# Moving a weight conversion ahead of the silu's low part on VectorE, and the second head's operand casts two steps later

## The chip, the cores and the metric

The kernel runs as one program on one core of one Trainium2 chip. The metric is device time in microseconds (us), the median of three runs. Inside the core five engines work side by side, each through its own instructions in order: TensorE (PE in the profile, with its weight loads as PEld), VectorE (DVE), ScalarE (ACT), GpSimd (POOL) and SyncE (SP). SyncE computes nothing; its line is the queue from which nearly all DMA transfers are issued. One engine waits for another through semaphores.

## The reference

Three parts in a chain, all in 32-bit floats (shapes: batch 2, 8 heads, 768 positions, head size 64; 1536 tokens of width 512):

```
q_bits = (q @ proj > 0);  k_bits = (k @ proj > 0)          # 6 bits each
mask   = bucket(q_bits) == bucket(k_bits)
attn   = softmax(where(mask, q @ k.T / 8, -1e9));  x = attn @ v
h = x @ w_in;  x = (h * sigmoid(h)) @ w_out                # 512 -> 2048 -> 512
tokens with x @ w_skip > 0 go to the best of 8 experts:
    x += gate * (relu(x @ w1[e]) @ w2[e])                   # 512 -> 1024 -> 512
```

## The kernel before, in words

**Split operands.** TensorE multiplies in a rounded 32-bit format. To keep precision a matrix is written as a high part (the rounded value) and a low part (what the rounding lost), and a product is taken as high x high + low x high + high x low. In the MLP a weight piece `wraw` of 128x1024 becomes `whi` (a cast on ScalarE, line 249) and `wlo` (a subtraction on VectorE, line 252).

**Attention.** Heads are worked in eight pairs. A pair has 12 steps, numbered m = 0 to 11 in the code (so the eighth step is m = 7): two halves of the queries ("units"), three blocks of 128 queries in each, two heads for each block, alternating. Step s issues, in order: scores `S` on TensorE (line 391; the operands are K1, K2, Q1, Q2), the first half of the transposes `T` of step s-2 (line 417) with ScalarE's copy `PT` (line 420), the row maximum `mx` and `bs` on VectorE (401, 403), the exponentials `P` on ScalarE (405), the product `pv` with the values (431), and the second half of the transposes with VectorE's copy (422). There are two score buffers, so `S` of step s waits until `P` of step s-2 has read its buffer.

While pair i is worked, the operands of pair i+1 are prepared. Two lists set by hand where: `PRE` (ahead of `P` in the step) and `POST` (at the step's end). For each head (0 or 1) there are six pieces: `kh` and `qa` are casts on ScalarE (lines 317 and 320) that write the high parts; `k2` and `qb` are DMA copies of those parts to the other half of the partitions, issued on SP (lines 312 and 314); `kl` and `ql` are subtractions on GpSimd (325, 330). The first pair has lists of its own (`i == 0`). Pair i+1's step 0 needs head 0, its step 1 needs head 1. SP's queue also carries, in this order: the mask rows (lines 355 and 360), and at each unit's end the round trip of the row sums: `r` written to `r_d` in DRAM (445), read back as `rb` by two broadcasts (448) that wait until that write has landed; then the next values `v` (289) and the raw q and k (283).

`em_r` (line 442) transposes a unit's reciprocal row sums on TensorE as `rT`; it stood at `k == 1`, right behind the second and before the third pair of `pv` products of that unit. For the last unit the VectorE work before it includes the first silu's low part.

**Weights for the MLP.** They arrive as 64-bit numbers and are converted in three steps (`convert`): ScalarE makes `u` (line 214, two pieces), VectorE shifts into `mag` (215, two), and VectorE then does four more passes, two into `mag` (219) and two into `wraw` (223). The first four blocks are converted during attention, in single pieces at steps 4, 9 and 11 of pairs 2 to 5 and in the last steps; blocks 4 to 15 in the MLP's first batch of tokens.

**MLP.** Tokens run in three batches of 512, and each batch over 16 blocks n of the inner width. Block n issues: the split of block n+1 (`whi`, `wlo`) with the start of the conversion of block n+2 (`u`, shift), then `em_h(n)` (12 matmuls into `ph` at line 619, silu `g` and its high part `gh` on ScalarE at 625 and 626, its low part `gl` on VectorE at 627), then the rest of the conversion of block n+2, then `em_out(n-1)` (12 matmuls into `o`, lines 653 and 662). All engines' orders are fixed by the order in which the program writes them; no scheduler moves them.

Of the kernel before, what the change touches and what calls it, by code (L numbers as in the profile page):

```python
# [25 lines left out]
def kernel(  # L26
# [16 lines left out]
    nc = tc.nc  # L43
# [190 lines left out]
    def split(i):  # L234
        assert next(splitting(i), "end") == "end"
# [28 lines left out]
    def attention(hook):  # L264
# [26 lines left out]
        def prep_alloc(i):  # L291
            pl = mainp if i % 2 else evp
            ops[i] = [pl.tile([P, 2, S], F32R, name=n, bufs=1) for n in ("Q1", "K1", "Q2")] + [K2s[i % 2]]
            mks[i] = (topp.tile([P, HQ], F32, name="ma"), topp.tile([P, HQ], F32R, name="mb"))
# [78 lines left out]
        units = [(i, qh) for i in range(B * NP) for qh in range(2)]  # L373
# [6 lines left out]
        def em_S(s, parts=(0, 1)):  # L380
            u, qt, hd = steps[s]
            i, qh = units[u]
            Q1, K1, Q2, K2 = ops[i]
            q0 = qh * HQ + qt * P
            if 0 in parts:
                st_S[s] = psS.tile([P, 2, 512], F32, tag="S", name="S", bufs=2)
            ps = st_S[s]
            for j in parts:
                q_, k_, n, first = ((Q1, K1, P, True), (Q2, K2, NK2, False))[j]
                for c in range(2):  # L390
                    nc.tensor.matmul(ps[:, c, 0:HQ], q_[0:n, hd, q0:q0 + P], k_[0:n, hd, c * HQ:(c + 1) * HQ],  # L391
                                     start=first, stop=not first)
# [33 lines left out]
        def em_PV(u, k):  # L426
            i, qh = units[u]
            if k == 0:
                st_pv[u] = psTV.tile([P, HQ], F32, tag="V", name="pv", bufs=1)
            for hd in range(2):  # L430
                nc.tensor.matmul(st_pv[u][hd * D:(hd + 1) * D], vts[i][:, k, hd], st_PT[u][:, hd, k],  # L431
                                 start=(k == 0), stop=(k == KT - 1))
# [45 lines left out]
        def em_busy(n):  # L478

            for _ in range(n):  # L480
                nc.tensor.matmul(bs, busy[:, 0:P], busy, start=True, stop=True)
# [21 lines left out]
        for j, ps in enumerate(direct):  # L503
# [6 lines left out]
            else:  # L510
# [14 lines left out]
        prep_op(1, 0, "scale", nc.scalar)  # L525
        nc.gpsimd.memset(K2s[1][D:D + 32].bitcast(F32), 0.0)

        PRE = [(1, 0, "kh", nc.scalar), (3, 0, "qa", nc.scalar), (5, 1, "kh", nc.scalar), (7, 1, "qa", nc.scalar)]

        POST = [(1, 0, "k2", None), (2, 0, "kl", nc.gpsimd), (3, 0, "qb", None), (4, 0, "ql", nc.gpsimd),  # L530
                (5, 1, "k2", None), (7, 1, "kl", nc.gpsimd), (7, 1, "qb", None), (9, 1, "ql", nc.gpsimd)]

        PRE, POST = ([ops_, [(x + 2, *op) for x, *op in ops_]] for ops_ in (PRE, POST))
        rbs, xs = {}, {}
        for s in range(NS + PU + 4):
            i, m = divmod(s, 2 * PU)
            nxt = i + 1 < B * NP
            if nxt and m == 0:
                prep_alloc(i + 1)
            if s < NS:  # L540
                em_S(s, (0, 1) if s else (1,))
            if 0 <= s - 2 < NS:
                em_T(s - 2, 0)
            for mm, *op in PRE[i == 0]:
                if nxt and mm == m:
                    prep_op(i + 1, *op)
            w, pm = divmod(s, PU)
            u, k = (w - 1, pm - 2) if pm >= 2 else (w - 2, pm + 4)
            pv = 0 <= u < len(units)

            if pv and k % 2:
                em_PV(u, k - 1)
                em_PV(u, k)
            if s < NS:
                em_soft(s)
            if s == 1:
                prep_op(0, 1, "k2", nc.scalar)
                prep_op(0, 1, "kl", nc.vector)
            if s < 2:
                em_busy(2)  # L560
            if 0 <= s - 2 < NS:
                em_T(s - 2, 1)
            if pv:
                if k == 0:
                    em_rc(u)
                if k == 1:
                    rbs[u] = em_r(u)
                if k == KT - 1:
                    xs[u] = em_out(u)
                if k == 3 and u:  # L570
                    em_x(u - 1, xs.pop(u - 1), rbs.pop(u - 1), nc.gpsimd)
            if nxt:
                if m == (1 if i else 5):
                    prep_proj(i + 1)
                if m == (2 if i else 6):
                    prep_mask(i + 1, nc.gpsimd if i else nc.scalar)
                for mm, *op in POST[i == 0]:
                    if mm == m:
                        prep_op(i + 1, *op)
                if m == (4 if i else 8):  # L580
                    prep_rows(i + 1)
                if m == 0 and i + 2 < B * NP:
                    prep_load(i + 2)
                if m == (9 if i else 11) and i + 2 < B * NP:
                    prep_op(i + 2, 0, "scale", nc.scalar)
                if m == 11 and i + 2 < B * NP:
                    load_v(i + 2)
                if m == 11 and i + 2 == B * NP:
                    top_st.close()
            if s == NS - 2 * PU:  # L590
                ev_st.close()
            hook(s - NS)
            if s == NS - 1:
                psS_st.close()
# [246 lines left out]
    with tc.manual_schedule():  # L841
# [17 lines left out]
        for n in range(N + 1):  # L859
            cv = convert(n + 2) if NEARLY <= n + 2 < NF else iter(())  # L860
            while cnt["spl"] < min(n + (3 if n >= NF else 2), N):

                sp = splitting(cnt["spl"], apart=True)
                next(sp)
                next(cv, None)
                next(sp, None)
            if n >= N - 2:
                while cnt["spl"] < NM + (1 if n == N - 2 else 3) and any(h[1] > 1 for h in homes):
                    split(cnt["spl"])
            if n < N:  # L870
                if n >= len(EARLY_H):
                    em_h(n)
                for _ in cv:
                    pass
            if n == NF - 2:
                pools["stg_st"].close()
                pools["gwb"], gwb_st = opened("gwb", side="right")
                pools["gwb_t"] = pools["gwb"].tile([P, NE + 1, DM], F32, name="gwb")
                nc.sync.dma_start(pools["gwb_t"].rearrange("p c d -> p (c d)"), gr.to_broadcast([P, (NE + 1) * DM]))
            if n == 3:  # L880
                cf = pools["xo"].tile([P, DM], F32, tag="x", name="cf", bufs=6)
                nc.sync.dma_start(cf[:, 0:consts.shape[1] - NC - P], consts[:, NC + P:])
            if n == 6:
                nc.vector.tensor_copy(cb, cf[:, 0:consts.shape[1] - NC - P])
            if n == 1:
                nc.sync.dma_start(tk, tok)
                nc.gpsimd.memset(gwc, 0.0)
                nc.sync.dma_start(gwc[:, :, 0:NE + 1], gw.rearrange("(k p) c -> p k c", p=P))
                z = pools["gwb0"] = sm.tile([P, NE * NTOK // P], F32, name="zid", bufs=1)
                nc.gpsimd.memset(z, float(DUMMY))  # L890
                nc.sync.dma_start(id_d.rearrange("(p r) c -> p (r c)", p=P), z)
                zx = sm.tile([P, DM // P], F32, name="zx", bufs=1)
                nc.gpsimd.memset(zx, 0.0)
                nc.sync.dma_start(x_d[NTOK:NTOK + 1].rearrange("o (p c) -> (o p) c", p=P), zx)
                nc.sync.dma_start(g_d[NTOK:NTOK + 1], zx[0:1, 0:1])
            if n >= 1:
                em_out(n - 1)
                b, f = items[n - 1]
                if f == NF - 1 and b + 1 < len(TILES):
                    todo.extend((t, c) for t in range(*TILES[b]) for c in range(NE + 1))  # L900
            if routing is not None and next(routing, "end") == "end":
                routing = None
            if n % NF:
                for j in range(4):
                    if todo:
                        logit(*todo.pop(0))
                        if not todo:
                            bb = n // NF - 1
                            if idx is None:
                                idx = ps_tile("idx", [P, 3], "O4")  # L910
                            routing = route(*TILES[bb], L[:, TILES[bb][0]:TILES[bb][1]], ps_tile("pr", [P, 512], "X"), idx)
# [49 lines left out]
        for t in range(t1 - t0):  # L961
            x = pools["xo"].tile([P, DM], F32, tag="x", name="x", bufs=6) if t < 2 else ep.tile([P, DM], F32, tag="eo", name="x")
# [280 lines left out]
```

## Time and profile before

| | |
|---|---|
| median of 3 runs | 639.28 us (638.69 to 642.12) |
| the profiled execution's own time | 640.85 us |
| its span, first to last instruction | 639.0 us |
| PE / DVE / ACT / POOL busy | 610.4 / 468.9 / 403.8 / 171.0 us |
| mean granted TensorE clock | 0.997 |

A row of the timeline has the start and the duration in us from the span's start, the engine, the line, the operation, output<-inputs, the count of merged instructions, and in brackets the idle time of the engine before it with what ended it. Matmuls are pipelined, so the next one may start before the modelled end of the last. In such rows the tiles K1 and K2 read `K`, and Q1 and Q2 read `Q`.

### The profile page before, as it was taken

The page shows a single profiled execution, that of the slowest core. Times are in us where ns is not written, and L with a number is a line of the kernel's source. Part 1 is how long each engine was busy: PE and PEld are TensorE (multiplying, and loading weights), DVE is VectorE, ACT ScalarE, POOL GpSimd, SP SyncE. Part 2 cuts the span into 40 slices and gives each one's busy share as a digit, 9 for nine tenths or more (in the row PEclk, how much of TensorE's full clock was granted, in tenths as well). Part 3 has the DMA queues.
Part 4 walks back from the last instruction along what each step waited for, and adds up shares of the span by engine and source line. Part 5 has one row for each costly group of instructions (what it writes and reads, how often), then busy time and mean ns, then how long its engine had stood idle before and what let it go on. Part 6 is the DMA issues. An engine that isn't in the chain of part 4 may idle for free.

```text
span 639.0 us, 9525 instructions
## 1 busy us (share of the span) xinstructions
PE 610.4 (96%) x3239; PEld 461.9 (72%) x3239; DVE 468.9 (73%) x861; ACT 403.8 (63%) x675; POOL 171.0 (27%) x261
## 2 busy tenths in 40 slices
PE   8899999999999999998899999999999988999996
PEld 3667676666767756776678888788887766788885
DVE  6867778788787665778776777447775568899992
ACT  6978788787887984454555333444433456788881
POOL 4437556383744142000000000020000035523201
PEclk9999999999999999999999999999999999999998
DMA  3532542534224124545443000007223258999920
GB/s 109 148 120 64 173 108 82 157 74 129 65 57 105 78 78 114 176 162 168 151 146 148 0 1 2 0 3 197 90 80 128 66 132 224 363 406 406 408 78 27
DMA packets 30978, 83.45 MB, mean 131 GB/s; under 512 B 6032, under 2 KB 9810, under 8 KB 30798
## 3 DMA queue, kind: packets, MB, share of 16 engines
q1 hardware_dynamic: 28834, 79.06, 38.5%
q0 software_dynamic: 1936, 3.65, 1.7%
q8 instruction: 26, 0.43, 0.3%
q14 instruction: 26, 0.21, 0.1%
q10 hardware_dynamic: 156, 0.10, 0.1%
HBM read 67.65 MB, written 8.50 MB: 119 GB/s over the span
## 4 chain that ended last, share of the span: by engine, by line
PE 74%; ACT 9%; DVE 7%; issue 4%; DMA 3%; POOL 1%; SPq 1%; POOLq 0%; DVEq 0%; ACTq 0%
PE ph L619 17%; PE o L662 10%; PE S L391 9%; PE pv L431 9%; PE T L417 8%; PE o L653 7%; PE eh L1059 5%; PE ey L1081 5%; ACT P L405 3%; ACT u L214 2%; DVE mag L219 2%; DVE mx L401 1%; PE tr L1037 1%; DVE wraw L223 1%; ACT K L317 1%
## 5 line engine op out<-in xcount | busy, mean ns | idle before, releaser
L249 ACT CAST whi<-wraw 128x1024 fp32r<-128x1024 f32 x100 | 102.7, 1050 | 45.0 <-DVE wraw L223 38.1
L252 DVE TENSOR_TENSOR wlo<-wraw,whi 128x1024 fp32r<-128x1024 f32 x100 | 119.6, 1222 | 11.5 <-ACT whi L249 10.5
L405 ACT ACTIVATE P<-S,bs 128x768 f32<-128x768 f32 x96 | 95.5, 994 | 26.0 <-DVE bs L403 23.2
L401 DVE TENSOR_REDUCE mx<-S 128x1 f32<-128x768 f32 x96 | 91.1, 949 | 14.2 <-PE S L391 11.8
L391 PE MATMUL S<-K,Q 88*128 88x384 f32 (+1 forms) x384 | 92.5, 362 | 7.8 <-ACT P L405 6.0
L625 ACT ACTIVATE g<-ph 128x512 f32<-128x512 f32 x48 | 28.5, 595 | 107.1 <-PE ph L619 93.7
L417 PEld LDWEIGHTS T<-ident,P 128*128 128x128 f32 x576 | 68.0, 140 | 30.9 <-ACT PT L420 18.6
L627 DVE TENSOR_TENSOR gl<-g,gh 128x512 fp32r<-128x512 f32 x48 | 33.3, 693 | 77.0 <-ACT gh L626 77.0
L417 PE MATMUL T<-ident,P 128*128 128x128 f32 x576 | 88.7, 277 | 0.2 <-ACT PT L420 0.2
L791 POOL DMA_INDIRECT id_d<-tk,slot x12 | 12.1, 1006 | 261.6 <-DVE pre L799 258.5
L391 PEld LDWEIGHTS S<-K,Q 88*128 88x128 f32 (+1 forms) x384 | 63.0, 191 | 16.0 <-ACT P L405 8.8
L431 PE MATMUL pv<-PT,v 128*64 128x384 f32 x384 | 72.5, 499 | 0.0
L422 DVE COPY PT<-T 128x384 f32<-128x384 f32 x85 | 47.0, 553 | 22.0 <-PE T L417 21.3
L619 PE MATMUL ph<-xhi,whi 128*128 128x512 f32 x192 | 54.4, 405 | 6.4 <-ACT whi L249 6.4
L420 ACT COPY PT<-T 128x384 f32<-128x384 f32 x107 | 50.6, 479 | 9.4 <-PE T L417 8.7
L619 PE MATMUL ph<-xlo,whi 128*128 128x512 f32 x192 | 52.3, 394 | 0.0
L619 PE MATMUL ph<-xhi,wlo 128*128 128x512 f32 x192 | 52.1, 393 | 0.0
L619 PEld LDWEIGHTS ph<-xhi,whi 128*128 128x128 f32 x192 | 34.6, 188 | 17.8 <-ACT whi L249 10.6
L675 DVE CUSTOM_DVE_ANT_0 junk<-x,gwb 128x512 bf16<-128x512 f32 x72 | 45.4, 686 | 0.0
L619 PEld LDWEIGHTS ph<-xlo,whi 128*128 128x128 f32 x192 | 36.1, 188 | 8.5
L619 PEld LDWEIGHTS ph<-xhi,wlo 128*128 128x128 f32 x192 | 36.1, 188 | 8.3
L431 PEld LDWEIGHTS pv<-PT,v 128*64 128x64 f32 x384 | 23.3, 136 | 25.5 <-issue 25.2
(177 smaller groups left out, 1049.9 us busy)
## 6 DMA issues: line engine op xcount, KB each, us to landing
wraw<-in_w_dram SPq DMA_DIRECT2D x64, 512.0 KB
w<-in_mw_dram SPq DMA_DIRECT2D x32, 512.0 KB
v<-in_vt_dram SPq DMA_DIRECT2D x8, 384.0 KB
rb<-r_d SPq DMA_DIRECT2D x32, 96.0 KB
out_dram<-x SPq DMA_DIRECT2D x12, 256.0 KB
x_d<-x SPq DMA_DIRECT2D x11, 256.0 KB
raw<-in_kT_dram SPq DMA_DIRECT2D x7, 384.0 KB
raw<-in_qT_dram SPq DMA_DIRECT2D x7, 384.0 KB
```

The lines of the kernel that those rows point to most:

```text
L249: nc.scalar.copy(hi[:, sl], t[:, sl])
L252: eng.tensor_tensor(lo[:, sl], t[:, sl], hi[:, sl].bitcast(F32), op=ALU.subtract)
L391: nc.tensor.matmul(ps[:, c, 0:HQ], q_[0:n, hd, q0:q0 + P], k_[0:n, hd, c * HQ:(c + 1) * HQ], start=first, stop=not first)
L401: nc.vector.tensor_reduce(mx[:, 0:1], ps[:, :, 0:HQ], axis=AX.XY, op=ALU.max, negate=True)
L405: nc.scalar.activation(pt.rearrange("p (a b) -> p a b", a=2), ps[:, :, 0:HQ], AF.Exp, bias=bs_[:, 0:1], scale=bs_[:, 1:2], accum_out=st_su ...
L417: nc.tensor.transpose(ps[:, j], pt[:, k * P:(k + 1) * P], ident)
L420: nc.scalar.copy(dst, ps)
L422: nc.vector.tensor_copy(dst, ps)
L431: nc.tensor.matmul(st_pv[u][hd * D:(hd + 1) * D], vts[i][:, k, hd], st_PT[u][:, hd, k], start=(k == 0), stop=(k == KT - 1))
L619: nc.tensor.matmul(p_[:, 0:c1 - c0], w[:, k * P:(k + 1) * P], x[:, k, t0 * P + c0:t0 * P + c1], start=(q == 0), stop=(q == len(ops3) - 1))
L662: nc.tensor.matmul(acc[t], g[:, (t - t0) * P:(t - t0 + 1) * P], w[:, DM:PIECE], start=(f == 0 and q == 0), stop=(f == NF - 1 and q == 2))
L675: nc.vector.tensor_tensor_reduce(junk, xts[t], pools["gwb_t"][:, c], op0=ALU.mult, op1=ALU.add, scale=1.0, scalar=0.0, accum_out=L[:, t, c ...
```

## The change

```diff
@@ the lists in attention @@
-        PRE = [(1, 0, "kh", nc.scalar), (3, 0, "qa", nc.scalar), (5, 1, "kh", nc.scalar), (7, 1, "qa", nc.scalar)]
+        PRE = [(1, 0, "kh", nc.scalar), (3, 0, "qa", nc.scalar), (7, 1, "kh", nc.scalar), (9, 1, "qa", nc.scalar)]
         POST = [(1, 0, "k2", None), (2, 0, "kl", nc.gpsimd), (3, 0, "qb", None), (4, 0, "ql", nc.gpsimd),
-                (5, 1, "k2", None), (7, 1, "kl", nc.gpsimd), (7, 1, "qb", None), (9, 1, "ql", nc.gpsimd)]
-        PRE, POST = ([ops_, [(x + 2, *op) for x, *op in ops_]] for ops_ in (PRE, POST))
+                (7, 1, "k2", None), (8, 1, "kl", nc.gpsimd), (9, 1, "qb", None), (10, 1, "ql", nc.gpsimd)]
+        PRE, POST = ([ops_, [(x + (1 if x < 5 else -1), *op) for x, *op in ops_]] for ops_ in (PRE, POST))
@@ the step loop @@
-                if k == 1:
+                if k == (1 if u + 1 < len(units) else 3):
                     rbs[u] = em_r(u)
@@ the MLP's loop over blocks @@
             if n < N:
+                for _ in cv:
+                    pass
                 if n >= len(EARLY_H):
                     em_h(n)
-                for _ in cv:
-                    pass
```

From the second pair on, head 1's K cast and copy move from step 5 to step 7 and its Q cast and copy from step 7 to step 9; the GpSimd subtractions move from 7 and 9 to 8 and 10. In the first pair all twelve entries of `PRE` and `POST` move one step earlier, and head 1's `kl` (9 to 7) and `ql` (11 to 9) two. For the last unit `em_r` moves behind the third pair of `pv` products. In the MLP the four remaining conversion passes are written ahead of `em_h`.

VectorE in the MLP's first batch, before: `w_3202` and `w_3252` are the two arrived pieces of one weight block, and the rows run from one block's last conversion passes to the next block's.

```order
L219 SCALAR_TENSOR_TENSOR mag<-u,mag 128x512 x2
L223 SCALAR_TENSOR_TENSOR wraw<-u,mag 128x512 x2
L215 TENSOR_SCALAR mag<-w_3202 128x512
L215 TENSOR_SCALAR mag<-w_3252 128x512
L252 TENSOR_TENSOR wlo<-wraw,whi 128x1024
L627 TENSOR_TENSOR gl<-g,gh 128x512
L219 SCALAR_TENSOR_TENSOR mag<-u,mag 128x512 x2
L223 SCALAR_TENSOR_TENSOR wraw<-u,mag 128x512 x2
```

The same place now; the pieces have other numbers.

```order
L215 TENSOR_SCALAR mag<-w_3183 128x512
L215 TENSOR_SCALAR mag<-w_3233 128x512
L252 TENSOR_TENSOR wlo<-wraw,whi 128x1024
L219 SCALAR_TENSOR_TENSOR mag<-u,mag 128x512 x2
L223 SCALAR_TENSOR_TENSOR wraw<-u,mag 128x512 x2
L627 TENSOR_TENSOR gl<-g,gh 128x512
L215 TENSOR_SCALAR mag<-w_3235 128x512
```

The four passes of lines 219 and 223 have changed places with `gl`; the other rows keep their order.

SP's queue in the third pair, around the end of step 9 (`K_852` and `Q_851` are the operands of the fourth pair, `r`, `r_d` and `rb` the row sums' round trip):

```order
 L312 DMA K_104<-K_852 64x768
+L445 DMA r_d<-r 6x128
+L448 DMA rb<-r_d 64x384 x2
 L314 DMA Q_851<-Q_851 64x768
-L445 DMA r_d<-r 6x128
-L448 DMA rb<-r_d 64x384 x2
 L289 DMA v<-in_vt_dram 128x768
 L283 DMA raw<-in_kT_dram 128x768
```

The copy of head 1's Q stood ahead of the round trip and stands behind it now, right in front of `v`; this repeats in six pairs. In the first pair it is the reverse: there the copy stood behind the round trip and is now ahead of the mask rows.

## Rows read from the trace of the kernel before

**Rows 1.** Busy time by stretch (us, engines' busy, clock, DMA share, GB/s)
```profile
288.00:304.00 16.00, 13.97 (x59) 10.50 (x58) 12.59 (x22) 7.87 (x12) 0.00 (x0) 1.00 0.47 158
448.00:464.00 16.00, 16.00 (x71) 13.10 (x70) 12.22 (x29) 6.51 (x9) 0.00 (x0) 1.00 0.31 99
```

**Rows 2.** TensorE's timeline in the MLP's first batch: starts of blocks
```profile
248.77 1.10 PE L619 MATMUL ph<-xhi,whi 128*128 128x512 f32 x4
...
265.48 1.10 PE L619 MATMUL ph<-xhi,whi 128*128 128x512 f32 x4
...
297.32 1.20 PE L619 MATMUL ph<-xhi,whi 128*128 128x512 f32 x4 [0.67 <-ACT whi L249]
...
335.42 1.08 PE L619 MATMUL ph<-xhi,whi 128*128 128x512 f32 x4
```

**Rows 3.** The chain of waits in that batch (start, us, what)
```profile
290.69 1.23 ACT u L214 x2
...
293.78 1.20 DVE mag L219 x2
...
296.22 0.03 ACT whi L249
...
297.18 1.23 ACT u L214 x2
```

**Rows 4.** VectorE's timeline over one block there
```profile
293.09 0.69 DVE L627 TENSOR_TENSOR gl<-g,gh 128x512 fp32r<-128x512 f32 x1 [1.05 <-ACT gh L626]
...
296.11 0.76 DVE L215 TENSOR_SCALAR mag<-w 128x512 int32<-128x512 int32 x2
297.31 1.23 DVE L252 TENSOR_TENSOR wlo<-wraw,whi 128x1024 fp32r<-128x1024 f32 x1 [0.44 <-ACT whi L249]
```

**Rows 5.** TensorE's timeline at the last unit's row sums
```profile
239.85 0.27 PE L442 MATMUL rT<-ident,sums 128*6 128x128 f32 x1 [1.00 <-DVE sums L436]
```

**Rows 6.** TensorE's timeline around the first pair's end
```profile
28.85 0.97 PE L391 MATMUL S<-K,Q 128*128 128x384 f32 x4 [1.21 <-ACT P L405]
...
39.34 0.94 PE L391 MATMUL S<-K,Q 128*128 128x384 f32 x4 [1.47 <-DMA Q<-Q]
```

**Rows 7.** SP's queue around the first pair's end
```profile
29.15 0.86 SPq L355 DMA_DIRECT2D Q<-mb  x1
...
36.12 0.58 SPq L314 DMA_DIRECT2D Q<-Q  x1
```

**Rows 8.** ScalarE's timeline in the first pair
```profile
24.88 0.99 ACT L405 ACTIVATE P<-S,bs 128x768 f32<-128x768 f32 x1 [0.81 <-DVE bs L403]
```

**Rows 9.** ScalarE's timeline in the third and fourth pair
```profile
83.50 0.83 ACT L320 CAST Q<-raw 64x768 fp32r<-64x768 f32 x1
...
88.74 0.99 ACT L405 ACTIVATE P<-S,bs 128x768 f32<-128x768 f32 x1 [0.35 <-DVE bs L403]
...
107.64 0.84 ACT L317 ACTIVATE K<-raw 64x768 fp32r<-64x768 f32 x1
108.51 0.99 ACT L405 ACTIVATE P<-S,bs 128x768 f32<-128x768 f32 x1
```

**Rows 10.** VectorE's timeline in the fourth pair
```profile
107.83 0.16 DVE L403 SCALAR_TENSOR_TENSOR bs<-mx 128x2 f32<-128x2 f32 x1
```

**Rows 11.** TensorE's timeline in the fourth pair
```profile
94.73 0.94 PE L391 MATMUL S<-K,Q 128*128 128x384 f32 x4
...
109.64 0.97 PE L391 MATMUL S<-K,Q 128*128 128x384 f32 x4 [0.63 <-ACT P L405]
```

**Rows 12.** SP's queue at the third pair's end
```profile
85.82 0.54 SPq L314 DMA_DIRECT2D Q<-Q  x1
...
92.42 0.54 SPq L289 DMA_DIRECT2D v<-in_vt_dram  x1
```

**Rows 13.** GpSimd's timeline at the first pair's end
```profile
31.60 2.26 POOL L330 TENSOR_TENSOR Q<-raw,Q 64x192 fp32r<-64x192 f32 x4 [1.58 <-DMA Q<-mb]
```

**Rows 14.** Busy time by stretch behind the first pair's Q copy
```profile
40.00:42.00 2.00, 2.00 (x14) 0.84 (x12) 1.12 (x2) 1.36 (x3) 0.00 (x0) 1.00 0.82 318
42.00:44.00 2.00, 2.00 (x17) 1.21 (x16) 1.18 (x2) 1.19 (x3) 0.00 (x0) 1.00 0.48 109
```

## The prediction

> **What bounds the kernel now.** I read the busy time by stretch first. TensorE is granted its full clock (1.00, the 2.4 GHz level) and is busy all of the time in the MLP's second batch, but 13.97 of 16.00 us in the first batch [rows 1], where the weights are converted. So a change there is worth what TensorE waits there, and elsewhere what it puts in TensorE's way.
>
> TensorE's timeline shows it at two paces. From 248.77 to 265.48 three blocks take 16.71 us, 5.57 each, with no wait. From 265.48 to 335.42 eleven blocks take 69.94 us; those in the middle wait 0.7 us for `whi` and take 6.49 [rows 2]. The chain of waits in that stretch leaves TensorE altogether: it goes round from `u` through the silu, `gl`, `mag` and `wraw` to `whi` and the next `u`, from 290.69 to 297.18, again 6.49 us [rows 3]. That is one loop over ScalarE and VectorE: a block's `whi` waits for the conversion, the conversion stands behind the earlier block's `gl`, and that `gl` waits for a `gh` that ScalarE does behind the `whi` of the block between. VectorE itself is not full: it idles 1.05 us before `gl` and 0.44 before `wlo` [rows 4].
>
> In attention TensorE is the bound, with two kinds of short waits that concern this change: `S` waits for `P` where ScalarE has too much in one step, and, once, `S` waits for a Q copy by DMA [rows 6, 11].
>
> **The MLP's order.** Nothing is added or removed; four passes go ahead of `gl`. The loop that is left runs `whi`, `wlo`, four passes, `whi`. From the start of `whi` to the start of `wlo` are 297.31 - 296.22 = 1.09 us, `wlo` takes 1.23, the four passes some 2.4 (two by 1.20, twice) [rows 3, 4]: 4.7 us. VectorE's whole work for a block is the same as now, 6.49 less its idle 1.05 and 0.44, so 5.0 us. Both are under TensorE's 5.57, so TensorE becomes the bound. Now `gl` stands in front of the next shifts and `wlo` when it waits for `gh`, but those have 0.5 us of room in each block and feed a block whose matmuls come more than one block later. Nor is `gl` itself late: the last third of `em_out` reads it after `em_out` of the block before, `em_h` of the block after and two thirds of its own matmuls, over 5 us. Eleven blocks at 5.57 are 61.3 us: 69.9 - 61.3 = 8.7 us less. The bounds: nothing, if another link holds the loop at 6.49; 8.7 if none does. I take 8.7, since the same blocks ran at 5.57 just before.
>
> **The last `em_r`.** TensorE idles 1.00 us for the row sums, whose two VectorE passes stand behind the first `gl` [rows 5]. Behind one more pair of products (about 1.5 us) they are done: 1.0 us less. The round trip behind it starts a little later; what waits for it is GpSimd, not TensorE, at that point.
>
> **The first pair.** Two gains. Head 1's Q copy was issued at 36.12, behind the row sums' round trip, and the second score of the next pair waited 1.47 us for it [rows 6, 7]; now it goes ahead of the mask rows, and has all their time to land. And the K cast (0.84 us, from [rows 9]) goes ahead of the exponential that starts at 24.88, where ScalarE idles 0.81 us [rows 8], and no longer delays the one behind it, for which a score waits 1.21 us [rows 6]: 0.8 of it goes. Together 2.3 us less. The other casts there move into steps in which ScalarE has as much work as before; I count them at nothing, and one exposed cast would cost 0.8.
>
> **The six other pairs.** The K cast leaves step 5. In four of them (pairs with a conversion piece at step 4) it delays an exponential: that starts at 108.51, and its `bs` is ready at 107.99 [rows 9, 10]. So it starts 0.52 earlier and the 0.63 wait of `S` shrinks by as much [rows 11]. It takes the place of the Q cast in step 7, nearly the same length (0.84 and 0.83), at no cost.
>
> The Q cast lands in step 9 ahead of `P` at 88.74, where ScalarE idles 0.35 us [rows 9]. With the 0.52 just won that covers 0.87, so the cast's 0.83 fits; in the two pairs without that gain `P`, and all behind it, come 0.83 - 0.35 = 0.48 later.
>
> Its copy is the price. It was issued at 85.82, 8.9 us ahead of the score that needs it, at 94.73; now it comes behind the round trip, in the place that `v` has, 92.42 [rows 11, 12]. How long it takes there the first pair shows, where the same copy stood behind the same two `rb` broadcasts and ahead of `v`: 39.34 - 36.12 = 3.22 us from issue to the score [rows 6, 7]. So the score starts at 95.64 instead of 94.73, 0.91 later, in four pairs, and 0.91 + 0.48 = 1.39 later in two: 3.6 + 2.8 = 6.4 us more. This already holds the 0.52 gained. At TensorE each is a wait of about 1.4 us, since without it the score would come at 94.21.
>
> How far can that duration be off? The quickest neighbour is a small DMA into Q: issued at 29.15, its reader started at 31.60, 2.45 us [rows 7, 13]. At 2.45 the price falls by 0.77 in each of six pairs, to 1.8 us. At the other end, the copy could be served together with all that is queued behind it; that traffic thins out a little past 42 [rows 14], some 6.1 us after the issue, 2.88 more for each pair, 23.7 us in all. I take 3.22, the row of the same transfer between the same neighbours.
>
> The Trainium skill's page "DMA: Bandwidth & Descriptors", section "Anatomy of one DMA", puts a transfer (on GpSimd's path) at about 2.0 us plus its bytes at 436 GB/s; for 192 KB that is an estimate of 2.4 us, by which the sum would be the first rival's. The first pair's 3.22 disagrees for this queue. Its section "Queues, rings and completion order" says that descriptors are consumed in ring order and that the completion comes after that engine's earlier writes; so the broadcasts ahead would hold the copy up, and `v` behind it would not. No row here separates the two.
>
> **The sum.** 8.7 + 1.0 + 2.3 - 6.4 = 5.6 us less. Behind the first batch TensorE is the bound up to the experts, and the experts' loads follow the program's progress, so the whole is carried to the end. The profiled execution took 640.85 us (span 639.0), which gives 635.2; it lay 1.57 above the median of 639.28, and against that the forecast is 633.6.
>
> **The rivals.**
> *The copy lands early.* At 2.45 us the pairs cost 1.8 instead of 6.4: 629.0. If it never delayed a score, the four 0.52 would be pure gain: 625.2. For it: the queue ahead is short. Against it: the first pair's row.
> *The low part becomes the new wait.* `gl`, now last in VectorE's line, blocks the shifts and `wlo` behind it, or the arrival of a weight piece, whose buffer is freed only by the shift, closes a new loop. If the blocks fall only half way, to 6.03, then 11 x 0.46 = 5.1 of the 8.7 are lost: 638.7. Against it: 5.0 us of VectorE work under 5.57.
> *The gains in attention do not come*, because `bs` or the mask rows, now behind the copy in the first pair, are late: 2.3 + 4 x 0.52 = 4.4 less, 638.0.
> *Slower: the copy waits for all that is queued around it.* Its place is the second score of six pairs. It eats the gain from a duration of 3.22 + 5.6/6 = 4.15 us on, makes the kernel slower by over 0.5% from 4.7 on, and at 6.1 gives 633.6 + 6 x 2.88 = 650.9. For it: `v`, raw k and raw q follow at once, and weight pieces in some pairs. Against it: they followed in the first pair too.
>
> **How the numbers follow.** The forecast 0.62, its own range 630.5 to 636.7 (half a microsecond either way for each copy); the early copy 0.16; the low part 0.09; no gains in attention 0.06; slower 0.07. The range 628.5 to 638.0 holds the forecast, most of the early copy, and most of the two middle cases. A measurement here tells about 0.5% from no change, so faster means under 636.1: nearly all of the forecast and the early copy, 0.78. Within 0.5%: the two middle cases and the forecast's upper edge, 0.15. Slower 0.07.
>
> **What would show it.** In the first MLP batch block starts should be 5.5 to 5.6 us apart throughout, and `whi` waits gone from TensorE. VectorE's idle time there should stand before `gl`, with the four passes ahead of it. At the second score of the pairs from the third on, TensorE should wait about 1.4 us for Q<-Q, six times; the waits for `P` in four pairs should be 0.1 instead of 0.63; the 1.47 and the 1.00 should be gone. The forecast is wrong if the blocks still stand at 6.4 us, or if those six waits are absent or above 2.4 us.

## The result, and the profile after

The changed kernel takes 635.2 us (median of 10 runs, 631.87 to 640.59), the kernel before 639.61 (10 runs, 638.46 to 643.69). The ratio is 0.9914, 95% interval 0.9887 to 0.9942. It is computed over the undisturbed runs and is not the quotient of the medians, which is 0.9931, or 4.4 us. On 639.6 us the ratio means 5.5 us less. The profiled execution took 633.52 us with a span of 631.7, 7.3 us under the span before.

**The MLP's first batch.** TensorE's timeline, at the starts of blocks 0, 2, 3, 4 and 16, answers to [rows 2]:

```profile
236.67 1.17 PE L619 MATMUL ph<-xhi,whi 128*128 128x512 f32 x4
...
249.64 1.09 PE L619 MATMUL ph<-xhi,whi 128*128 128x512 f32 x4
...
255.75 1.20 PE L619 MATMUL ph<-xhi,whi 128*128 128x512 f32 x4 [0.40 <-ACT whi L249]
...
261.41 1.10 PE L619 MATMUL ph<-xhi,whi 128*128 128x512 f32 x4
...
327.96 1.10 PE L619 MATMUL ph<-xhi,whi 128*128 128x512 f32 x4
```

From block 2 to block 16 are 327.96 - 249.64 = 78.32 us, before 335.42 - 248.77 = 86.65: 8.33 less. Behind block 3 no wait is left; twelve blocks from 261.41 take 66.55, 5.55 each. One wait is new, 0.40 at block 3.

VectorE's timeline over one block, which answers to [rows 4], with one earlier wait ahead of it:

```profile
286.89 0.43 DVE L215 TENSOR_SCALAR mag<-w 128x512 int32<-128x512 int32 x1 [1.09 <-DMA w<-in_mw_dram]
...
290.77 0.68 DVE L627 TENSOR_TENSOR gl<-g,gh 128x512 fp32r<-128x512 f32 x1
291.38 0.75 DVE L215 TENSOR_SCALAR mag<-w 128x512 int32<-128x512 int32 x2
292.05 1.22 DVE L252 TENSOR_TENSOR wlo<-wraw,whi 128x1024 fp32r<-128x1024 f32 x1
293.18 1.29 DVE L219 SCALAR_TENSOR_TENSOR mag<-u,mag 128x512 int32<-128x512 int32 x2
294.39 1.28 DVE L223 SCALAR_TENSOR_TENSOR wraw<-u,mag 128x512 int32<-128x512 int32 x2
295.60 0.68 DVE L627 TENSOR_TENSOR gl<-g,gh 128x512 fp32r<-128x512 f32 x1
```

From `gl` to `gl` are 4.83 us without a gap: VectorE's whole work for a block, less than TensorE's 5.55. Busy time in the first stretch of [rows 1], same columns:

```profile
288.00:304.00 16.00, 16.00 (x71) 12.97 (x70) 16.00 (x27) 10.18 (x16) 0.00 (x0) 1.00 0.60 208
```

TensorE is now busy all of it, as it was in the second batch before. VectorE shows 16.00 too, and yet it is not the bound: it works ahead of TensorE's need as far as the weights have arrived, and these 16 us lie behind a late piece (the 1.09), after which it catches up. The reader should not take "busy all the time" for "sets the pace"; the work per block tells.

**Attention.** TensorE's timeline at scores. The first two rows answer to [rows 6] (28.85 and 39.34 before; the second score of the second pair has lost its wait). The row at 93.50 is one of the six waits for the moved copy; 78.56 and 79.13, the transposes and the score behind them, stand in the first pair that has a conversion piece at step 4 ("hook pair" below); 107.98 holds the one wait for `P` that remains of the four like that in [rows 11]:

```profile
27.97 0.97 PE L391 MATMUL S<-K,Q 128*128 128x384 f32 x4 [0.22 <-ACT P L405]
...
36.73 0.95 PE L391 MATMUL S<-K,Q 128*128 128x384 f32 x4
...
78.56 0.82 PE L417 MATMUL T<-ident,P 128*128 128x128 f32 x6
79.13 0.95 PE L391 MATMUL S<-K,Q 128*128 128x384 f32 x4
...
93.50 0.94 PE L391 MATMUL S<-K,Q 128*128 128x384 f32 x4 [0.93 <-DMA Q<-Q]
...
107.98 0.97 PE L391 MATMUL S<-K,Q 128*128 128x384 f32 x4 [0.21 <-ACT P L405]
```

SP's queue at the end of the third pair, which answers to [rows 12]. The copy is issued at 90.39, ahead of `v`, and its score starts at 93.50:

```profile
87.97 0.29 SPq L445 DMA_DIRECT2D r_d<-r  x1
89.20 1.13 SPq L448 DMA_DIRECT2D rb<-r_d  x2
90.39 0.59 SPq L314 DMA_DIRECT2D Q<-Q  x1
91.07 0.54 SPq L289 DMA_DIRECT2D v<-in_vt_dram  x1
```

The waits by group, for TensorE (us in total, times, the longest):

```profile
PE S L391 <- DMA Q<-Q: 6.5, 6, 1.6
PE S L391 <- ACT P L405: 3.0, 5, 1.0
```

TensorE's timeline of the kernel before at block 0, which the next table needs:

```profile
234.40 1.18 PE L619 MATMUL ph<-xhi,whi 128*128 128x512 f32 x4
```

Where the 7.3 us come from, stretch by stretch:

| stretch | before | after | difference |
|---|---|---|---|
| start to the first pair's score [rows 6] | 28.85 | 27.97 | -0.88 |
| to the second score of the second pair | 10.49 | 8.76 | -1.73 |
| to block 0 of the MLP | 195.06 | 199.94 | +4.88 |
| block 0 to block 2 (holds the last `em_r`) | 14.37 | 12.97 | -1.40 |
| block 2 to block 16 | 86.65 | 78.32 | -8.33 |
| block 16 to the end | 303.58 | 303.74 | +0.16 |

### The profile page after: what moved, and what is told of

Read it like the earlier page. It is cut to its first block, busy times and chain, and to the rows that moved or that the text cites. A ratio compares the mean times of both kernels' runs of the same rounds, so it can differ in the third digit from the quotient of the medians.

```text
span 631.7 us, 9542 instructions
## 1 busy us (share of the span) xinstructions
PE 607.9 (96%) x3239; PEld 462.4 (73%) x3239; DVE 469.5 (74%) x861; ACT 404.4 (64%) x675; POOL 175.5 (28%) x261
## 4 chain that ended last, share of the span: by engine, by line
PE 76%; DMA 5%; ACT 5%; DVE 4%; POOL 4%; issue 3%; SPq 1%; POOLq 0%; DVEq 0%; ACTq 0%
PE ph L619 20%; PE o L662 13%; PE o L653 7%; PE S L391 7%; PE eh L1060 7%; PE pv L431 6%; PE ey L1082 6%; PE T L417 6%; DMA Q<-Q 3%; ACT P L405 2%; POOL Q L330 2%; DVE mx L401 2%; PE tr L1038 1%; POOL K L325 1%; DMA r_d<-r 1%
## 5 line engine op out<-in xcount | busy, mean ns | idle before, releaser
L330 POOL TENSOR_TENSOR Q<-raw,Q 64x192 fp32r<-64x192 f32 x64 | 38.3, 626 | 21.2 <-ACT Q L320 18.3
```

Source lines behind the costliest of these rows:

```text
L330: eng.tensor_tensor(Q2[0:D, hd, c], qs[r, c], Q1[r, hd, c].bitcast(F32), op=ALU.subtract)
```

## Experiments

Two theories stood at the start. The first: the MLP's gain is TensorE's pace with the conversion's loop opened; the lists cost, because in six pairs the Q copy stands behind the round trip, and nothing else in them does. The rival: part of the MLP's gain or of the lists' cost is something else: a loop that is only half open, or a copy that is slow because of the traffic that follows it. All kernels below were compared with the kernel before on the same chip (medians 638.3 and 639.1 there).

**1. The MLP's order alone.** The kernel before, with this edit and nothing else:

```diff
             if n < N:
+                for _ in cv:
+                    pass
                 if n >= len(EARLY_H):
                     em_h(n)
-                for _ in cv:
-                    pass
```

> The kernel before with the MLP's reordering alone (four conversion passes ahead of the silu's low part); lists and last row sums as before. Theory: the parts add up, so the first MLP batch runs at TensorE's pace from its third block on, 5.55 us a block, and the whole comes 8.7 us under the kernel before, some 631. It lies then below the changed kernel, whose lists in attention cost 2.3 us up to the MLP. Rival: the gain came with the shifted attention work (weights that arrive at other times), and the reordering alone gives 4 to 5 us.

Measured: 628.93 us (628.56 to 631.33), ratio 0.9848, interval 0.982 to 0.9877, so 9.7 us less. TensorE's starts of blocks 2, 3 and 16:

```profile
246.43 1.09 PE L619 MATMUL ph<-xhi,whi 128*128 128x512 f32 x4
...
251.98 1.10 PE L619 MATMUL ph<-xhi,whi 128*128 128x512 f32 x4
...
324.12 1.09 PE L619 MATMUL ph<-xhi,whi 128*128 128x512 f32 x4
```

Block 2 to block 16 takes 77.69 us, 8.96 less than before, and block 3 follows by 5.55 with no wait. One edit of the three beats the whole change: the other two together lose time. The waits of attention are still those of before: 1.4 us for one Q copy, 1.0 for the row sums, 0.6 for `P` in each of the four hook pairs.

**2. The lists alone.** The kernel before, with the change's `PRE` and `POST` and no other edit:

```diff
-        PRE = [..., (5, 1, "kh", nc.scalar), (7, 1, "qa", nc.scalar)]
+        PRE = [..., (7, 1, "kh", nc.scalar), (9, 1, "qa", nc.scalar)]
...
-                (5, 1, "k2", None), (7, 1, "kl", nc.gpsimd), (7, 1, "qb", None), (9, 1, "ql", nc.gpsimd)]
+                (7, 1, "k2", None), (8, 1, "kl", nc.gpsimd), (9, 1, "qb", None), (10, 1, "ql", nc.gpsimd)]
```

> The kernel before with the two lists in attention alone. Theory: six waits of about 1.1 us of the second score for the Q copy, against 2.6 us won in the first pair and about 0.9 in each of three or four pairs; the first MLP block starts 2.3 us later than before, and the whole is 2.3 us slower, some 641.9. Rival: a slower attention is taken back later, since the weights' loop in the first MLP batch has its own pace; then the end is within 0.5 us of before.

Measured: ratio 1.0043, interval 1.0018 to 1.0068, so 2.7 us more, 1.1 to 4.3 (median 642.62). Right in sign and size. Six waits for the copy again, but one of 3.00 us, and the `whi` waits of the MLP untouched:

```profile
PE S L391 <- DMA Q<-Q: 8.1, 6, 3.0
...
PE ph L619 <- ACT whi L249: 6.4, 10, 0.8
```

SP's queue ahead of that longest wait, and TensorE's score:

```profile
57.81 0.29 SPq L445 DMA_DIRECT2D r_d<-r  x1
61.20 1.13 SPq L448 DMA_DIRECT2D rb<-r_d  x2
62.38 0.59 SPq L314 DMA_DIRECT2D Q<-Q  x1
```

```profile
65.40 0.93 PE L391 MATMUL S<-K,Q 128*128 128x384 f32 x4 [3.00 <-DMA Q<-Q]
```

The copy itself took its usual time, 65.40 - 62.38 = 3.02. It was issued late: the write of `r_d` took 61.20 - 57.81 = 3.39 us to land, against 1.23 in the queue shown above for the changed kernel, and the copy stands in line behind the broadcasts that wait for it. Traffic did not hold the write; the busy time by stretch has the DMA engines all but idle then (the last two columns, DMA share and GB/s):

```profile
58.00:60.00 2.00, 2.00 (x14) 1.33 (x15) 1.90 (x4) 1.90 (x5) 1.92 (x4) 1.00 0.04 10
```

Why it landed late stays open. But the new place has a second price, which the prediction left out: the copy inherits whatever delays the round trip. And more was lost behind the wait. From 66.62 to 70.03 us the granted clock was 0.50, the 1.2 GHz level; the eight `pv` products there took 2.83 us, in the changed kernel 1.51. TensorE's row, and the busy time by stretch:

```profile
66.59 2.83 PE L431 MATMUL pv<-PT,v 128*64 128x384 f32 x8
```

```profile
67.00:70.00 3.00, 3.00 (x11) 0.97 (x7) 0.49 (x2) 2.36 (x5) 0.00 (x0) 0.50 0.75 235
```

The late score came 4.61 us after the one before it, where 1.36 is undisturbed, and the next one 5.52 after the late one, where the changed kernel takes 3.90. Together 4.9 us were lost there, in the changed kernel 1.2.

**3. The Q copy put ahead of the round trip.** The changed kernel, with one DMA moved; all casts stay where the change put them:

```diff
-                ... (9, 1, "qb", None), (10, 1, "ql", nc.gpsimd)]
+                ... (10, 1, "ql", nc.gpsimd)]
...
+            if nxt and m == (9 if i else 8):
+                prep_op(i + 1, 1, "qb", None)
             if pv:
```

> The changed kernel, with head 1's Q copy at step 9 issued ahead of the row sums' round trip instead of behind it; the cast stays in step 9. Theory (SyncE's order makes the copy late): the six waits for the Q copy fall from 6.5 us to under 0.5, the gross delay of 7.9 us goes, and the kernel comes some 7 us below the changed one, about 628. Rival (the cast at step 9 is too late by itself, or the copy takes longer among other traffic): waits of 0.5 to 1 us in each pair stay, and the gain is at most 3 us.

Measured: 623.81 us (623.56 to 627.21), ratio 0.9765, interval 0.9735 to 0.9795, so 15.0 us less than before. SP's queue at the third pair's end has the copy in front again:

```profile
83.38 0.51 SPq L314 DMA_DIRECT2D Q<-Q  x1
84.63 0.29 SPq L445 DMA_DIRECT2D r_d<-r  x1
```

No score waits for a copy any more; of TensorE's two groups of score waits one is left:

```profile
PE S L391 <- ACT P L405: 3.4, 5, 1.3
```

From the third score to block 0 are 227.79 - 12.10 = 215.69 us, against 236.67 - 14.36 = 222.31 in the changed kernel: 6.62 less, which is what the copy's place cost. It is less than the 7.9 by which the six scores came late in the changed kernel (next section): in four pairs that score still starts 1.65 to 1.72 us after the one before it, where 1.36 is undisturbed, with `P` as the last thing that it needs, and these 1.2 us stay. The expectation was some 7 us. Each ratio taken on its own kernel before, the gains are 15.0 and 5.5 us, 9.5 apart, with some 1.8 either way on each. The two spans are 9.7 apart; 2.3 of that stand ahead of the third score, which no edit explains (last section), and 0.8 behind block 0.

**4. The later pairs' head 1 at steps 6 and 8.** The changed kernel; instead of moving the copy apart, its cast and copy come one step earlier:

```diff
-        PRE = [..., (7, 1, "kh", nc.scalar), (9, 1, "qa", nc.scalar)]
+        PRE = [..., (6, 1, "kh", nc.scalar), (8, 1, "qa", nc.scalar)]
...
-                (7, 1, "k2", None), (8, 1, "kl", nc.gpsimd), (9, 1, "qb", None), (10, 1, "ql", nc.gpsimd)]
+                (6, 1, "k2", None), (7, 1, "kl", nc.gpsimd), (8, 1, "qb", None), (9, 1, "ql", nc.gpsimd)]
```

(The first pair keeps the steps that the change gave it.)

> The changed kernel, with head 1's casts of the later pairs at steps 6 and 8 (copies there too, so the Q copy stands ahead of the round trip of step 9), as the changed first pair has them. Theory: no waits for the Q copy, and the K cast away from step 5 still frees most of the waits for the exponentials: 7 us below the changed kernel, about 628, like the variant with the copy ahead. Rival: ScalarE's extra casts at steps 6 and 8 make new waits of scores for exponentials, 0.3 to 0.6 us in each pair, and the gain shrinks to 4 us.

Measured: 623.71 us (621.86 to 625.29), ratio 0.9758, interval 0.9728 to 0.9788. The copy's waits are gone and no other came in their place: TensorE's scores wait for `P` alone, 3.3 us in 5 waits.

So the K cast need only leave step 5; the eighth and tenth steps were one too many. By its median it can't be told apart from experiment 3. The trace tells more: from the third score to block 0 it takes 225.84 - 12.09 = 213.75 us, 1.94 less than experiment 3, and the second score of those four pairs comes after 1.36 us again.

**5. The last row sums by another queue.** Experiment 4, with the last unit's round trip issued from ScalarE's queue, past the weight loads on SP:

```diff
+        q = nc.sync if u + 1 < len(units) else nc.scalar    # for r_d and rb, in em_r
```

> The variant with the later pairs' casts at steps 6 and 8, with the last unit's round trip of row sums issued from ScalarE's queue instead of SyncE's, where it stood behind three weight loads. Theory (the moved row sums cost GpSimd's last products 4 us by that queue, and so the fourth MLP block 0.5 us): the read back is issued some 3 us earlier, the fourth block follows the third by 5.55 us instead of 6.1, no wait for whi is left at TensorE in the first batch, and the whole is 0.5 us faster, which only the trace can tell. Rival: the round trip is slow because of the traffic of those loads, and from the other queue it lands no earlier.

In the changed kernel that round trip sits between weight loads on SP; its rows, then GpSimd's and ScalarE's behind it:

```profile
235.77 8.33 SPq L194 DMA_DIRECT2D w<-in_mw_dram  x3
244.20 0.29 SPq L445 DMA_DIRECT2D r_d<-r  x1
248.26 1.09 SPq L448 DMA_DIRECT2D rb<-r_d  x2
```

```profile
251.65 1.16 POOL L464 TENSOR_TENSOR x<-x,rb 128x192 f32<-128x192 f32 x2 [11.07 <-DMA rb<-r_d]
...
254.65 1.05 ACT L249 CAST whi<-w 128x1024 fp32r<-128x1024 f32 x1 [6.30 <-POOL xlo L468]
```

The three issues of loads hold the queue until 244.10, while `r` is ready at 242.91. It is not their transfers that hold it: an issue waits until VectorE's shift has freed a weight buffer, the longest 4.3 us, as the queue's own waits show.

```profile
SPq L194 <- DVE mag L215: 7.8, 3, 4.3
```

Then the write needs 4.06 us to land, GpSimd's `x` and `xlo` come late, and ScalarE's `whi` of block 3, behind them in line, starts at 254.65. Before, with block 0 2.27 us earlier, the write was issued at 240.44 and that `whi` started at 250.72:

```profile
240.44 0.28 SPq L445 DMA_DIRECT2D r_d<-r  x1
```

In experiment 5 the trip runs on ScalarE's queue, and the same `whi`:

```profile
232.17 0.53 ACTq L446 DMA_DIRECT2D r_d<-r  x1
233.44 1.14 ACTq L449 DMA_DIRECT2D rb<-r_d  x2
...
242.02 1.05 ACT L249 CAST whi<-w 128x1024 fp32r<-128x1024 f32 x1 [4.43 <-POOL xlo L469]
```

The write lands in 1.27 us, and block 3 follows block 2 by 244.43 - 238.88 = 5.55; in experiment 4 it was 244.90 - 238.81 = 6.09. The wait is gone, as expected. Whether the landing of 4.06 us belongs to SP's queue or to the moment, no run separates: the DMA engines' busy share was 0.44 over those 4 us, and 0.05 where experiment 5's write ran. Measured: 621.91 us (621.34 to 625.51), ratio 0.974, interval 0.9705 to 0.9775. The half microsecond against experiment 4 shows in the trace alone; the intervals overlap. This is the lowest median of all, under both kernels.

**6. Only two of the four passes ahead.** The kernel before; `convert` pauses between its two `mag` and its two `wraw` passes, and only the first two go ahead of `em_h`:

```diff
+                next(cv, None)      # the two mag passes
                 if n >= len(EARLY_H):
                     em_h(n)
                 for _ in cv:        # the two wraw passes
                     pass
```

> The kernel before, in which only the first two of the four conversion passes (into mag) go ahead of the silu's low part; the two into wraw stay behind it. Theory (a loop of whi, u, silu, low part, passes): its length falls by the two passes, 1.2 us, from 6.49 to 5.3, under TensorE's 5.56, so nearly all of the gain comes: blocks 5.6 us apart, the whole 8 to 9 us under before. Rival (whi waits for the place of wraw in VectorE's line, which is still behind the low part, and the low part waits for TensorE): half of the gain or none, blocks at 6.0 to 6.5 us, the whole at most 5 us under before.

Measured: 632.27 us (628.91 to 633.69), ratio 0.9873, interval 0.9838 to 0.9909, so 8.1 us less. VectorE's timeline over a block:

```profile
288.22 0.69 DVE L629 TENSOR_TENSOR gl<-g,gh 128x512 fp32r<-128x512 f32 x1
288.83 1.29 DVE L225 SCALAR_TENSOR_TENSOR wraw<-u,mag 128x512 int32<-128x512 int32 x2
...
291.24 1.23 DVE L254 TENSOR_TENSOR wlo<-wraw,whi 128x1024 fp32r<-128x1024 f32 x1 [0.36 <-ACT whi L251]
```

Block 2 to block 16 takes 328.31 - 250.62 = 77.69, to the hundredth the same as experiment 1. VectorE still waits 0.36 for `whi` here, but the loop is under TensorE's pace, and what is under it costs nothing. So the loop had to be shortened only to 5.55, and half of the passes do that. That the gain goes with the number of passes moved, falls. The whole gained 8.1 us here and 9.7 in experiment 1; the intervals overlap, and in this trace attention, which the edit does not touch, lost 1.8 us more around the first pair's end, most of it at a granted clock of 0.50 (last section).

**7. Nothing behind the copy.** The changed kernel, with the loads that follow the copy at a pair's end put off: `v` to step 3, the raw q and k to step 2 of the next pair.

```diff
-            if m == 0 ...: prep_load(i + 2)
+            if m == 2 ...: prep_load(i + 2)
...
-            if m == 11 ...: load_v(i + 2)
+            if m == 3 and i: load_v(i + 1)
```

> The changed kernel, with the loads of values and of raw q and k moved away from behind the Q copy of step 9 (values to step 3, raw to step 2 of the next pair). Nothing but weight pieces follows the copy then. Theory A (the copy is held up by the two broadcasts ahead of it in the queue): it still takes 3.0 to 3.3 us from issue to the score, and the six waits stay at 6 to 7 us. Theory B (it shares the transfer engines with what follows it): it takes about 2.4 us, the waits fall to 2 us or less, and the spread of the times narrows from 8 us to 4.

Measured: 633.52 us (632.17 to 634.95), ratio 0.9904, interval 0.9872 to 0.9936. SP's queue at the third pair's end, now with no load right behind the copy, and TensorE's score:

```profile
90.48 0.59 SPq L314 DMA_DIRECT2D Q<-Q  x1
```

```profile
94.00 0.94 PE L391 MATMUL S<-K,Q 128*128 128x384 f32 x4 [1.34 <-DMA Q<-Q]
```

Issue to score takes 3.24, 3.52, 3.35, 3.08, 3.13 and 3.17 us in the six pairs, with the loads behind it 3.08 to 3.63; the waits add up to 6.6, in the changed kernel to 6.5. The traffic behind the copy does not matter to it, and that rival falls. Its times spread over 2.8 us, narrower than the changed kernel's 8.7, as Theory B had it; with 6 executions against 10 and the same waits, that alone shows nothing. Whether its 3.2 us are its own, or owed to the two broadcasts ahead of it, no run tells apart.

## Why the prediction was right, and where it was off

The forecast was 633.6 us against 639.28, 5.6 less; measured are 5.5 less by the ratio. Point by point:

- **The MLP's order, -8.7.** Right in mechanism and size. Of the 8.33 between blocks 2 and 16, 0.54 went to the late block 3 (next point), so the order itself gave 8.87; alone it gave 8.96. The loop over ScalarE and VectorE was the bound, TensorE is it now. One sign was foretold wrongly: VectorE was to idle in front of `gl` in each block. It shows no gap there; its 0.7 us of room for each block go into working ahead, until a weight piece is late.
- **The last `em_r`, -1.0.** Here a step failed: "what waits for it is GpSimd, not TensorE, at that point." The products ran 1.40 earlier, but the round trip fell behind weight loads on SP, the last of which waits for a shift on VectorE, GpSimd came late, and ScalarE's `whi` of block 3 stands behind what GpSimd releases. TensorE waited 0.40 there, and block 3 came 255.75 - 249.64 = 6.11 after block 2 instead of 5.57: 0.54 lost, 0.86 kept. Experiment 5 gives the 0.54 back. The prediction asked who waits for the delayed transfer, but not who waits for the one that waits.
- **The first pair, -2.3.** Measured -0.88 - 1.73 = -2.61. The 1.47 is gone, and the K cast freed 0.88 where 0.8 was forecast.
- **The six other pairs, +6.4.** Right mechanism, size too high: +4.88. The copies took 3.08, 3.11, 3.63, 3.18, 3.25 and 3.08 us from issue to score: a mean of 3.22, exactly the first pair's row [rows 6, 7]. The scores came 1.16, 1.18, 1.86, 1.26, 1.34 and 1.13 us later, together 7.9, where the sum had 8.5 before the relief. The term that was mis-sized is the relief in the four hook pairs: 0.52 each, from how far `P` stood behind `bs` in the fourth pair [rows 9, 10]. Measured are 0.88, 0.42, 0.86 and 0.86, 3.0 instead of 2.1. The 0.42 is the fourth pair's. There two shifts (line 215, 0.85 us) stand ahead of `mx` on VectorE, and `P` now waits 0.47 for `bs`; in the other three pairs one shift does (0.43 to 0.45), and `P` starts without a wait. The row was read from the one pair of the four that had least to gain. The rows of the first hook pair before also show how a wait of 0.63 could cost 0.88:

```profile
80.20 0.82 PE L417 MATMUL T<-ident,P 128*128 128x128 f32 x6
81.65 0.98 PE L391 MATMUL S<-K,Q 128*128 128x384 f32 x4 [0.63 <-ACT P L405]
```

  The score started 81.65 - 80.20 = 1.45 us behind the start of the transposes; now it starts 79.13 - 78.56 = 0.57 behind it, 0.25 ahead of their modelled end at 79.38. The idle time in a bracket is counted from that end, so each such wait costs about 0.25 us more than its bracket says: 6.5 us idle and 7.9 lost at the six copies, 1.47 and 1.73 in the first pair.
- **The rivals.** That the copy waits for everything around it (650.9) was the one that would have reversed the sign. Experiment 7 closes it. The early copy (629.0) is closed by the six durations, none of them near 2.45. That the low part becomes the new wait fell with experiment 1. That the gains in attention do not come fell with the changed kernel's own rows: -2.61 in the first pair, 3.0 in the four hook pairs.

The Trainium skill's page "DMA: Bandwidth & Descriptors" was weighed in the prediction at two places. Its section "Queues, rings and completion order" has descriptors consumed in ring order, from which the prediction read that what stands behind a transfer does not hold it up; experiment 7 agrees, with 3.08 to 3.52 us where no loads follow. From its section "Anatomy of one DMA", on GpSimd's path, an estimate of 2.4 us came for the copy; the six copies, at 3.22 from issue to the start of the score and behind two broadcasts, disagree for this queue.

Term by term the trace's -7.3 stands against the forecast's -5.6 like this: the MLP 0.2, the first pair 0.3 and the six pairs 1.5 better, the last `em_r` 0.1 and everything behind block 16 0.2 worse. The timed ratio, 3.7 to 7.2 us, lies around the forecast and just under the trace; which part of that is chance in the two profiled executions stays open.

## What to carry to other kernels

When an instruction is moved past a DMA that waits for something, all that the wait can ever be belongs to the price, not only the wait of the usual case: behind experiment 2's one late write of row sums TensorE lost 4.9 us instead of 1.2, with the copy as quick as ever. An issue that waits for a buffer holds up what is written behind it in the same queue (experiment 5). A relief that is to count in four places is read in all four, not in one. If a bundle of edits gains, time each alone: here one edit gained 9.7 us, the second lost 2.7, and the second, with one transfer put back in front, is a gain as well. An order that opens a loop needs to bring it only under the next bound; what goes beyond that buys nothing (experiment 6).

## What was unexpected of the hardware

**The start at two speeds.** The third score starts at 14.36 in the changed kernel (14.41 before, 14.44 and 14.28 in experiments 6 and 7) and at 12.09 to 12.55 in the others, though the same is computed up to there. TensorE's first products, in the changed kernel:

```profile
4.28 4.02 PE L495 MATMUL pd<-raw,ct 64*32 64x384 f32 x6
```

and in experiment 4:

```profile
4.25 2.53 PE L495 MATMUL pd<-raw,ct 64*32 64x384 f32 x6
```

The same products take 1.6 times as long, though TensorE was busy without a gap from 2 to 8 us in both. The granted clock reads 1.00, the 2.4 GHz level, in both stretches, but that reading says nothing here: the trace has no clock record yet, and the view prints 1.00 where none stands. The first record, of 1.00, begins at 10.41 us in the changed kernel and at 5.12 in experiment 4. In the four traces with the later start it begins at 10.13 to 10.55 us, in the other five at 4.12 to 5.22, and in all nine the pace changes there: a product of line 481 takes 0.53 us ahead of it and 0.33 behind it. Kernels with the lists of before and with those of after are in both groups, so the change does not decide it, and what does, no run shows. The Trainium skill's page "TensorE: Matmul & The Clock Gate", section "Part 1: The HAM clock gate (the "warmup" mystery)", has the engine at 1.2 GHz until it has been busy for some time; the slower rows ahead of the first record fit that. Two profiled spans can differ by 2.3 us through it alone. That is why the table of stretches is used here; the two kernels in it both had the later start.

**A slower clock behind a long wait.** Twice the granted clock fell to 0.50 in the middle of attention: in experiment 2 at 66.62 us, behind the wait of 3.00 for the late copy, and in experiment 6 from 41.27 to 44.69, behind a wait of 1.69 for the first pair's copy, which the edit there does not touch. In experiment 6 the score behind the late one came 5.48 us after it, in the kernel before 3.90. Waits of up to 1.6 us in attention in the other traces, and one of 1.8 among the experts in experiment 7, had no such stretch behind them. What decides it, these runs do not show.

**A write's landing.** The same 3 KB write of row sums landed in 1.23 us in most places, in 3.39 with the DMA engines all but idle (experiment 2), and in 4.06 with a weight load issued just ahead of it (the changed kernel's last one). From ScalarE's queue it took 1.27 at that last place, with the DMA engines all but idle.
